# Windowed attention, mixture of experts and MLP: local values loaded once, with a product in two passes over alternating key halves

## Chip, cores and metric

One core of a Trainium2 chip. The metric is the device time of one execution in microseconds; of several runs the median is given.

## What is computed

Four batches of 576 positions, eight heads of 64. In heads 0 to 3 a query sees its own key and the 31 before it; in heads 4 to 7 every fourth position back, 32 of them (`rel` is query minus key position):

```
scores = scale * q @ k.T
mask   = (0 <= rel < 32)                  if h < H // 2
         (0 <= rel < 128, rel % 4 == 0)   otherwise
x      = softmax(where(mask, scores, -1e9)) @ v        # heads side by side: (B, S, 512)
```

Behind it come a causal attention of four experts, of which each token takes the two with the highest gate logits, and a layer norm with an MLP (512 to 2048 to 512, relu) and a residual sum:

```
for e in range(4): out += w_e * softmax(causal(scale * (x@wq[e]) @ (x@wk[e]).T)) @ (x@wv[e]) @ wo[e]
y = out + relu(norm(out) * g @ w_ch1) @ w_ch2
```

All data are float32.

## The kernel before

**Local attention** works by head pair (two heads, one in each half of the 128 partitions), 4 pairs for each of 4 batches, 16 in all. Pairs 0 and 1 are plain, pairs 2 and 3 dilated; a dilated head is split into its four classes of position modulo 4, each of 144 positions, which then look like the plain case.

For each pair `load_qk` (line 330) loads queries and keys into two tiles `nat`, `load_v` (line 354) the values into a tile `vt`, and `turned_qk` (line 432) turns queries and keys by matmuls with an identity (`ptr`, line 451) into `qT` and `kT`, with 32 zero columns ahead of the keys. Some of these tiles lie in `x2a`, the space that later holds the tokens.

Queries go in blocks of 32. A block sees 64 keys: its own 32 and the 32 before. `scores` (line 497) writes for each block a matmul with a mask (lines 513 to 518) and one of queries with those 64 keys (line 526), on eight tiles of 64 by 32 of TensorE's array at a time. `window` (line 532) takes maxima and exponentials, `local` (line 555) sums and normalises them on VectorE or GpSimd (line 578), turns them by matmuls (`ppt`, line 585) into `pT`, and multiplies them with the values (`po`, line 612) on four tiles of 64 by 64: one matmul for each block and head, with the 64 values that the block sees as weights and its 32 columns of `pT` streamed:

```
nc.tensor.matmul(pos[u][z, o:o + m], vv, pT[y, p0:p0 + m], start=True, stop=True)
```

For that, `vt` holds the values of every block with those of the block before it: each value is loaded twice. `u` is 0 or 1, for the first ten and the last eight or ten blocks. `rounded` (line 619) then splits the result into `xh` (ScalarE, line 633) and `xl` (VectorE, line 635).

**Behind it** `value_tile` multiplies with the experts' value weights (`pv`, line 659), `project` with query and key weights (`pp`, line 760), `attend` is the causal attention (`s` in lines 832 to 835, `ppt` in 908, `py` in 927 and 929), `out_proj` (`pwo`, line 985) gives the tokens. `attention_weights` (line 287) splits each weight that has landed into a rounded part (ScalarE, line 294) and a rest (GpSimd, line 296). The MLP (`phid`, line 1213, `pout`, line 1235) takes some 450 us at the end.

**The order** on every engine is set ahead of time by the kernel's own planner, `run_chains`: each piece of work is a chain that yields its operations with a supposed duration (`yield op("PE", 1050.0, ...)`), its need of a buffer (`acq`) or of an earlier result (`key`); what could start first by these suppositions is issued first, by rank where equal. SP issues all loads in the order of `all_loads` (line 411): after batch 0's queries, keys and values come the weights, then batch 1.

Of the kernel before, what the change touches and what calls it, by code (L numbers as in the profile page):

```python
# [23 lines left out]
def windowed_attention_moe_mlp(  # L24
# [37 lines left out]
    LEAN = 0.0  # L62

# [38 lines left out]
    HOME = list(range(8)) + [9, 10, 11, 12, 8, 13]  # L102
    LENT = 11
# [5 lines left out]
    def x2(ti):  # L109
        if ti < NTA:  # L110
            return x2a[:, HOME[ti]]
# [16 lines left out]

    mask = win.tile([P, NS, 2 * W], BF16, name="mask")
    nc.gpsimd.memset(mask[:, 1], 0.0)  # L130
    for x in range(4):
        m = mask[W * x:W * x + W, 1]
        nc.gpsimd.affine_select(out=m, in_=m, pattern=[[1, 2 * W]], compare_op=ALU.is_gt,
                                fill=NEG, base=0, channel_multiplier=-1)
        nc.gpsimd.affine_select(out=m, in_=m, pattern=[[-1, 2 * W]], compare_op=ALU.is_ge,
                                fill=NEG, base=W, channel_multiplier=1)
    for x in (0, 2, 3, 4):
        nc.vector.tensor_copy(mask[:, x], mask[:, 1])
    for x in range(4):
        nc.vector.memset(mask[W * x:W * x + W, x % 2 * 2, 0:W], NEG)  # L140
# [165 lines left out]
    places.update(nat=[0.0] * 2, vt=[(0.0, 8), (0.0, LENT), (0.0, 0), (0.0, 0)], qT=[0.0] * 2, xh=[0.0] * XB)  # L306
# [23 lines left out]
    def load_qk(b, hp, engines="SS"):  # L330
# [9 lines left out]
        for x, src in enumerate((q, k)):  # L340
            if lent:
                nat = x2a[:, 4 * hp - 4 + 2 * x:4 * hp - 2 + 2 * x].rearrange("p a n -> p (a n)")
            else:
                nat = win.tile([P, 2 * DM], F32, tag="nat", name="nat", bufs=2)
# [9 lines left out]
    def load_v(b, hp, engines=("SP",)):  # L354
# [3 lines left out]
        if home:  # L358
            vt = x2a[:, home:home + 3].rearrange("p a n -> p (a n)")[:, :4 * NS * D]
        else:  # L360
            vt = win.tile([P, 4 * NS * D], F32, tag="vt", name=f"vt{b}_{hp}", bufs=2)
        yield op("POOL", 1000.0 if dil else 250.0, [t])
        vs, jobs = v[b, h0], []
        if not dil:
            vt = vt.rearrange("p (i h d) -> p i h d", i=2 * NS, h=2)
            nc.gpsimd.memset(vt[0:W, 0], 0.0)
            jobs.append((16.0, vt[W:2 * W, 0], v[b, h0:h0 + 2, 0:W].rearrange("h p d -> p h d")))
            for u, i0, n in ((0, 1, 9), (1, 0, 8)):
                for h in range(2):
                    jobs.append((16.0 * n, vt[64 * u:64 * u + 64, i0:i0 + n, h],  # L370
                                 bass.AP(tensor=vs.tensor, offset=vs.offset + (h * S + (10 * u + i0 - 1) * W) * D,
                                         ap=[[D, 2 * W], [W * D, n], [1, D]])))
        else:
            vt = vt.rearrange("p (i h n) -> p i h n", i=NS, h=2)
            for u in range(NU):
                nc.gpsimd.memset(vt[64 * u:64 * u + W, 0], 0.0)
                nc.gpsimd.memset(vt[64 * u + W:64 * u + 2 * W, 4], 0.0)
            for u in range(NU):
                y, o = 64 * u, 2 * u * D
                for h in range(2):  # L380
                    jobs.append((70.0, vt[y:y + 2 * W, 1:4, h],
                                 bass.AP(tensor=vs.tensor, offset=vs.offset + h * S * D + o,
                                         ap=[[4 * D, 2 * W], [4 * W * D, 3], [1, 2 * D]])))
                for i, w0, w1 in ((0, W, 2 * W), (4, 0, CLS - 3 * W)):
                    jobs.append(((w1 - w0) * 0.7, vt[y + w0:y + w1, i],
                                 bass.AP(tensor=vs.tensor, offset=vs.offset + 4 * ((i - 1) * W + w0) * D + o,
                                         ap=[[4 * D, w1 - w0], [S * D, 2], [1, 2 * D]])))
        tv = 0.0
        for x, (kb, dst, src) in enumerate(jobs):
            ns = 470.0 if dil else 580.0  # L390
# [40 lines left out]

    def turned_qk(b, hp):
# [4 lines left out]
        qT = win.tile([P, S], F32, tag="qT", name=f"qT{b}_{hp}", bufs=2)  # L437
        kT = win.tile([P, W + S], F32, tag="kT", name=f"kT{b}_{hp}", bufs=2)
        yield op("POOL", 130.0, [tq])
        nc.gpsimd.memset(kT[:, 0:W], 0.0)  # L440
# [4 lines left out]
        for x in range(4):  # L445
# [11 lines left out]
            dst = kT[:, W:] if x > 1 else qT  # L457
# [30 lines left out]
    def piece(dil, u, s, c):  # L488

        i = 2 * NS * u + 2 * s + c  # L490
        if not dil:
            return W * i, W, 2 * W, 2 * W * s + W * c
        r, g = divmod(i, 5)
        m = min(W, CLS - W * g)
        return CLS * r + W * g, m, m + W, CLS * (r % 2) + W * g

    def scores(b, hp):
# [8 lines left out]
        t = yield op("PE", 1200.0, [tq, ta], "eighths")  # L506
# [13 lines left out]
        for s in range(NS):  # L520
            for u, z, c in tiles:
                n = parts(dil, u)
                if s < n:
                    q0, mq, mk, _ = piece(dil, u, s, c)
# [3 lines left out]
        give("qT", t)  # L528
        PSC[b, hp] = banks, psv
# [25 lines left out]
    def local(b, hp):  # L555
# [41 lines left out]
        t = yield op("PE", 1050.0, ends + [ta, tv], "quarters")  # L597
        for s in range(NS):
            for c in range(2):
                for u in range(NU):  # L600
                    if s >= parts(dil, u):
                        continue
                    _, m, _, o = piece(dil, u, s, c)
                    y = slice(64 * u, 64 * u + 64)
                    for h, z in enumerate(HALVES):
                        p0 = P * s + side(u, z).start + W * c
                        if dil:
                            r, g = divmod(2 * NS * u + 2 * s + c, 5)
# [717 lines left out]
```

## Time and profile before

| | |
|---|---|
| median of 3 runs | 730.36 us (729.48 to 731.95) |
| profiled execution | 730.35 us |
| its span | 728.6 us |
| TensorE busy | 702.5 us, 96% |
| VectorE, ScalarE, GpSimd busy | 506.0, 287.1, 156.6 us |
| moved by DMA | 45.49 MB |

The span goes from the first to the last instruction of that execution. Busy time of TensorE counts matmuls that overlap as one stretch. A float32 matmul leaves two records in the trace. The granted clock is 1.00 at 2.4 GHz and 0.50 at 1.2 GHz.

### The profile page before, as it was taken

Reading aid. Unit: us, or ns where it says so; the run is one execution under the profiler, and the core shown is the slowest. Engines: PE = TensorE matmul, PEld = TensorE weight load, DVE = VectorE, ACT = ScalarE, POOL = GpSimd, SP = SyncE. Lnnn points to the kernel's source line nnn. Section 1 sums busy time; section 2 is a strip of 40 time slices with the busy share of each in tenths; the row PEclk is TensorE's granted clock in tenths of the full one; section 3 lists DMA queues with packets and bytes.
Section 4 is the critical chain, followed back from the end, with each engine's and each line's share of the span. In section 5 each row is a group of like instructions: output and inputs, shape, how many; then the busy total and the mean of one; then the engine's idle time right before and its main releaser. Section 6 shows DMA issues by size and latency. Waiting matters only on the chain.

```text
span 728.6 us, 16135 instructions
## 1 busy us (share of the span) xinstructions
PE 702.5 (96%) x6483; PEld 592.5 (81%) x6483; DVE 506.0 (69%) x1206; ACT 287.1 (39%) x814; POOL 156.6 (21%) x209
## 2 busy tenths in 40 slices
PE   6977999999999899999999999999999999999997
PEld 4876998998898878778888888888888888888886
DVE  4526789976978889994958984684674864854343
ACT  3445567756766665962412231221221211311100
POOL 3352101010100204430404341240330420410000
PEclk9577799999999999999999999999999999999999
DMA  9699165125612111110101220020110110100123
GB/s 156 126 177 165 36 132 112 50 52 104 117 23 68 38 42 47 37 48 0 58 1 59 73 72 30 29 61 26 58 58 0 59 58 2 57 1 0 58 88 115
DMA packets 89275, 45.49 MB, mean 62 GB/s; under 512 B 65648, under 2 KB 84592, under 8 KB 89200
## 3 DMA queue, kind: packets, MB, share of 16 engines
q1 hardware_dynamic: 89200, 44.46, 26.4%
q8 instruction: 51, 0.84, 0.5%
q14 instruction: 24, 0.20, 0.1%
HBM read 37.37 MB, written 4.72 MB: 58 GB/s over the span
## 4 chain that ended last, share of the span: by engine, by line
PE 85%; DVE 9%; SPq 2%; ACT 2%; DMA 1%; issue 1%; POOL 0%; DVEq 0%; ACTq 0%; POOLq 0%
PE pout L1235 27%; PE phid L1213 27%; PE pp L760 6%; PE pv L659 4%; PE po L612 3%; PE pwo L985 3%; PE ptr L451 2%; PE ppt L908 2%; PE py L929 2%; SPq L322 2%; PE s L526 2%; PE py L927 1%; PE s L832 1%; PE s L833 1%; PE ppt L585 1%; DMA x2a<-in_k_dram 1%
## 5 line engine op out<-in xcount | busy, mean ns | idle before, releaser
L1213 PE MATMUL phid<-xn,wp 128*128 128x512 f32 (+1 forms) x960 | 219.9, 372 | 0.0
L1235 PE MATMUL pout<-wp,ht 128*128 128x512 f32 x864 | 217.9, 394 | 0.0
L1213 PEld LDWEIGHTS phid<-xn,wp 128*128 128x128 f32 x960 | 168.3, 188 | 34.1 <-issue 0.2
L1235 PEld LDWEIGHTS pout<-wp,ht 128*128 128x128 f32 x864 | 160.7, 188 | 36.2 <-issue 0.3
L1244 DVE SCALAR_TENSOR_TENSOR x2a<-pout,rstd,x2a 128x512 f32<-128x512 f32 x124 | 92.2, 748 | 55.8 <-PE pout L1235 54.9
L1218 ACT ACTIVATE ht<-phid 128x512 fp32r<-128x512 f32 (+1 forms) x80 | 44.5, 556 | 215.3 <-PE phid L1213 215.3
L1220 DVE SCALAR_TENSOR_TENSOR ht<-phid,ht 128x512 fp32r<-128x512 f32 (+1 forms) x80 | 50.7, 634 | 60.5 <-ACT ht L1218 60.1
L1087 POOL TENSOR_TENSOR d_pw<-d_pw,d_t 128x512 f32<-128x512 f32 x32 | 41.4, 1294 | 217.2 <-DVE d_pw L1084 185.7
L1099 POOL TENSOR_TENSOR wp<-d_pw,wp 128x512 fp32r<-128x512 f32 x32 | 42.6, 1330 | 40.7 <-ACT wp L1097 40.7
L1071 ACT ACTIVATE d_sq<-ws 128x512 f32<-128x512 f32 x32 | 21.6, 676 | 52.9 <-DVE d_pw L1090 29.2
L578 POOL TENSOR_TENSOR sc<-sc,rs 128x384 f32<-128x384 f32 (+2 forms) x20 | 14.6, 738 | 106.2 <-DVE rs L571 53.8
L1097 ACT CAST wp<-d_pw 128x512 fp32r<-128x512 f32 x32 | 20.0, 624 | 40.6 <-DVE d_pw L1090 33.1
L848 ACT ACTIVATE Pp<-s,nm 128x448 f32<-128x448 f32 (+3 forms) x64 | 30.6, 478 | 13.2 <-DVE nm L846 10.6
L245 ACT COPY pT<-ppt 128x256 f32<-128x256 f32 (+3 forms) x63 | 27.0, 434 | 17.3 <-PE ppt L908 9.2
L832 PE MATMUL s<-KH,SQ 128*128 128x288 f32 (+4 forms) x96 | 31.5, 333 | 0.3 <-ACT G L245 0.2
L1090 DVE SCALAR_TENSOR_TENSOR d_pw<-d_sq,d_pw 128x512 f32<-128x512 f32 x32 | 22.0, 688 | 13.9 <-POOL d_pw L1087 13.8
L846 DVE TENSOR_REDUCE nm<-s 128x1 f32<-128x448 f32 (+3 forms) x64 | 26.2, 416 | 6.3 <-PE s L835 5.9
L1244 DVE SCALAR_TENSOR_TENSOR x2b<-pout,rstd,x2b 128x512 f32<-128x512 f32 x32 | 24.0, 749 | 9.3 <-PE pout L1235 9.1
L908 PE MATMUL ppt<-ident,Pp 128*128 128x128 f32 x160 | 29.2, 285 | 1.1 <-DVE xn L1175 0.8
L833 PE MATMUL s<-klz,SQ 128*128 128x288 f32 (+4 forms) x96 | 28.7, 303 | 0.0
L1077 DVE SCALAR_TENSOR_TENSOR d_t<-ws,d_t 128x512 int32<-128x512 int32 x32 | 27.6, 861 | 0.5
L551 ACT ACTIVATE sc<-s,mx 128x64 f32<-128x64 f32 x97 | 21.7, 330 | 14.8 <-DVE mx L542 11.9
(171 smaller groups left out, 1284.4 us busy)
## 6 DMA issues: line engine op xcount, KB each, us to landing
ws<-in_moe_w_ch_dram SPq DMA_DIRECT2D x32, 512.0 KB, 3.6
nat<-in_q_dram SPq DMA_DIRECT2D x12, 288.0 KB, 3.8
nat<-in_k_dram SPq DMA_DIRECT2D x12, 288.0 KB, 4.3
out_dram<-x2a SPq DMA_DIRECT2D x12, 256.0 KB, 2.1
KH<-KH SPq DMA_DIRECT2D x32, 72.0 KB, 2.7
vt<-in_v_dram SPq DMA_DIRECT2D x12, 144.0 KB, 4.2
vt<-in_v_dram SPq DMA_DIRECT2D x12, 128.0 KB, 5.5
x2a<-in_v_dram SPq DMA_DIRECT2D x16, 96.0 KB, 4.2
```

What stands on the lines that cost most here:

```text
L760: nc.tensor.matmul(pp[:, :HS], ws[:, c, pr_ * P:(pr_ + 1) * P], xs[:, c, cs], start=n == 0, stop=n == 3 * KC - 1)
L832: nc.tensor.matmul(ps[:m, :z - a], SQ[ee][:, q0:q0 + m], KH[ee][:, a:z], start=True, stop=False)
L833: nc.tensor.matmul(ps[:m, :z - a], SQ[ee][:, q0:q0 + m], KL[ee][:, a:z], start=False, stop=not end)
L848: nc.scalar.activation(Pt[:m, :n], pss[0][:m, :n], AF.Exp, bias=nm[:m, ee:ee + 1], accum_out=sm[:m, ee:ee + 1])
L908: nc.tensor.transpose(pt[:, P * (j - 1):P * j], Ps[ee][:, k0:k0 + P], ident)
L1087: nc.gpsimd.tensor_tensor(pf, pf, t1.bitcast(F32), op=ALU.add)
L1099: nc.gpsimd.tensor_tensor(lo, pf, hi.bitcast(F32), op=ALU.subtract)
L1213: nc.tensor.matmul(ph[:, :n_tok], ws[:, c * P:(c + 1) * P], xs[c], start=n == 0, stop=n == 3 * KC - 1)
L1218: nc.scalar.activation(hh[:, :n_tok], ph[:, :n_tok], AF.Relu)
L1220: nc.vector.scalar_tensor_tensor(hl[:, :n_tok], ph[:, :n_tok], 0.0, hh[:, :n_tok].bitcast(F32), op0=ALU.max, op1=ALU.subtract)
L1235: nc.tensor.matmul(po, a_[:, sl], w_, start=n == 0, stop=n == 3 * len(fs) - 1)
L1244: nc.vector.scalar_tensor_tensor(x2(i), po, rstd[:, i:i + 1], x2(i), op0=ALU.mult, op1=ALU.add)
```

## The change

Values are loaded once: `vt` holds, for the plain pairs, slots of 64 positions (for `u` = 1 beginning two blocks early), and for the dilated ones three slots for each class. So a block of 32 keys lies in partitions 0 to 31 of a half if its number is even, in 32 to 63 if odd. The scores put the 64 keys of a block in the order that fits this: for even blocks the two groups of 32 are swapped by a reversed read of `kT`, and the masks are built to match. The product becomes two passes, one over even key blocks and one over odd, which add up in PSUM: each matmul has one block of 32 keys as its weights (both heads' 64 value columns, or in the odd pass pieces of 32) and streams the two query blocks that see it, 64 columns.

`qT` and `kT` become two lasting pairs with the zero columns written once; `nat` gets a third tile; `vt` is smaller, and two more of its places lie in `x2a`, which loses its permutation `HOME`. The planner's suppositions change with it: 900 for 1200 (scores), 850 for 1050 (product), and those of the issues.

```
+    VW = 6 * P
...
-    HOME = list(range(8)) + [9, 10, 11, 12, 8, 13]
-    LENT = 11
+    LENT = 12
...
-    places.update(nat=[0.0] * 2, vt=[(0.0, 8), (0.0, LENT), (0.0, 0), (0.0, 0)], qT=[0.0] * 2, xh=[0.0] * XB)
+    places.update(nat=[0.0] * 3, vt=[(0.0, 8), (0.0, 10), (0.0, LENT), (0.0, 0), (0.0, 0)], qT=[0.0] * 2, xh=[0.0] * XB)
...
-            vt = vt.rearrange("p (i h d) -> p i h d", i=2 * NS, h=2)
-            nc.gpsimd.memset(vt[0:W, 0], 0.0)
-            jobs.append((16.0, vt[W:2 * W, 0], v[b, h0:h0 + 2, 0:W].rearrange("h p d -> p h d")))
-            for u, i0, n in ((0, 1, 9), (1, 0, 8)):
+            vt = vt[:, :NS * 2 * D].rearrange("p (i h d) -> p i h d", i=NS, h=2)
+            for u in range(NU):
                 for h in range(2):
-                    jobs.append((16.0 * n, vt[64 * u:64 * u + 64, i0:i0 + n, h],
+                    jobs.append((80.0, vt[64 * u:64 * u + 64, :, h],
...
-            vt = vt.rearrange("p (i h n) -> p i h n", i=NS, h=2)
-            for u in range(NU):
-                nc.gpsimd.memset(vt[64 * u:64 * u + W, 0], 0.0)
-                nc.gpsimd.memset(vt[64 * u + W:64 * u + 2 * W, 4], 0.0)
+            vt = vt.rearrange("p (i h n) -> p i h n", i=3, h=2)
             for u in range(NU):
                 y, o = 64 * u, 2 * u * D
                 for h in range(2):
-                    jobs.append((70.0, vt[y:y + 2 * W, 1:4, h],
+                    jobs.append((45.0, vt[y:y + 2 * W, 0:2, h],
...
-                for i, w0, w1 in ((0, W, 2 * W), (4, 0, CLS - 3 * W)):
-                    jobs.append(((w1 - w0) * 0.7, vt[y + w0:y + w1, i],
+                jobs.append((11.0, vt[y:y + CLS - 4 * W, 2],
...
+    QKT = [(win.tile([P, S], F32, name=f"qT{x}"), win.tile([P, W + S + W // 2], F32, name=f"kT{x}")) for x in range(2)]
...
-                    nc.tensor.matmul(psv[u][k:k + mq, s, :mk], qT[z, q0:q0 + mq], kT[z, q0:q0 + mk],
+                    keys = kT[z, q0:q0 + 2 * W].rearrange("p (a w) -> p a w", a=2)
+                    nc.tensor.matmul(psv[u][k:k + mq, s], qT[z, q0:q0 + mq], keys[:, ::-1] if swap else keys,
                                      start=False, stop=s == n - 1)
...
-        t = yield op("PE", 1050.0, ends + [ta, tv], "quarters")
+        t = yield op("PE", 850.0, ends + [ta, tv], "halves")
+        for odd in range(2):
...
+                    for g in range(odd - 2 if odd and u and not dil else odd, n, 2):
+                        kk = min(W, CLS - W * g) if dil else W
+                        sl = g // 2 if dil else g // 2 + u
+                        jobs[u].append((sl, r, kk, OW * r + W * max(g, 0), at[max(g, 0):g + 2]))
+            for x in range(max(map(len, jobs))):
                 for u in range(NU):
...
+                    y0 = 64 * u + W * odd
+                    dw = W if odd else D
+                    for d0 in range(0, 2 * D, dw):
...
+                        nc.tensor.matmul(pos[u][d0:d0 + dw, o:o + W * len(at)], vv, pp, start=not odd and not x,
+                                         stop=bool(odd) and x == len(jobs[u]) - 1)
```

The planner orders much anew. Two places are shown.

ScalarE, batch 0, where the key weights are cast (`wkh`, then `wqh`), before:

```order
L245 COPY pT<-ppt 128x384 x2
L245 COPY pT<-ppt 128x256
L294 CAST wkh<-ws_att 128x256 x3
L633 CAST xh_138<-po 128x2x144 x2
L294 CAST wkh<-ws_att 128x256
L294 CAST wqh<-ws_att 128x256 x2
L633 CAST xh_138<-po 128x2x144 x2
L294 CAST wqh<-ws_att 128x256 x2
```

and now:

```order
L255 COPY pT<-ppt 128x384
L255 COPY pT<-ppt 128x256
L304 CAST wkh<-ws_att 128x256
L255 COPY pT<-ppt 128x384
L304 CAST wkh<-ws_att 128x256 x2
L255 COPY pT<-ppt 128x256
L304 CAST wkh<-ws_att 128x256
L304 CAST wqh<-ws_att 128x256
L655 CAST xh_160<-po 128x2x144 x2
L304 CAST wqh<-ws_att 128x256 x3
L655 CAST xh_160<-po 128x2x144 x2
```

The casts of the key weights stood ahead of the rounding (`xh`) of the third pair, with all copies of `pT` done; now they stand between the copies of `pT`, and the first query weight ahead of that rounding.

TensorE, batch 1. Before, from the end of the second pair's scores on:

```order
L526 MATMUL s_1101<-kT_1_947,qT_1_946 32x64 x4
L585 MATMUL ppt<-ident,sc_132 128x128 x5
L612 MATMUL po<-pT,vt_0_819 64x32 x36
L451 MATMUL ptr<-ident,x2a 128x72 x16
L585 MATMUL ppt<-ident,sc_133 128x128 x3
```

Now a group of `ptr` (sixteen, of the third pair) and that pair's scores follow the second pair's scores directly, and then come:

```order
L782 MATMUL pp<-xh_160,wqh 128x288
L782 MATMUL pp<-xl_161,wqh 128x288
L782 MATMUL pp<-xh_160,wql 128x288
L456 MATMUL ptr<-ident,nat 128x72 x4
L590 MATMUL ppt<-ident,sc_154 128x128 x3
L456 MATMUL ptr<-ident,nat 128x72 x4
L590 MATMUL ppt<-ident,sc_155 128x128 x3
L590 MATMUL ppt<-ident,sc_154 128x128 x2
L456 MATMUL ptr<-ident,nat 128x72 x4
L590 MATMUL ppt<-ident,sc_155 128x128 x2
```

The transposes of the exponentials (`ppt`) followed the scores at once, with the product behind them; now the third pair's transposes and scores and six projection matmuls (`pp`) stand between, and the fourth pair's `ptr` among the `ppt`.

## Rows read from the trace of the kernel before

**Rows 1.** Busy time by stage: window, length, busy (instructions), granted TensorE clock, DMA, GB/s

```profile
0.00:50.00 50.00, 38.03 (x784) 31.90 (x785) 20.56 (x54) 20.97 (x63) 20.18 (x60) 0.73 0.88 151
50.00:110.00 60.00, 55.55 (x976) 50.67 (x976) 42.78 (x137) 35.55 (x122) 12.67 (x30) 0.85 0.64 117
110.00:240.00 130.00, 128.89 (x2243) 114.16 (x2242) 110.50 (x374) 88.50 (x299) 13.47 (x33) 1.00 0.36 73
```

**Rows 2.** Waits of TensorE, 0 to 110 us: total, times, longest

```profile
PE po L612 <- DVE xl L635: 4.1, 1, 4.1
PE ppt L585 <- POOL sc L578: 2.5, 2, 2.2
PE ptr L451 <- DMA x2a<-in_q_dram: 2.3, 1, 2.3
```

**Rows 3.** All engines by time around 42 us: start, length, idle before, releaser

```profile
40.01 1.49 ACT L294 CAST wkh<-ws_att 128x256 fp32r<-128x256 f32 x3 [3.74 <-DMA ws_att<-in_moe_wk_dram]
...
41.41 1.19 ACT L633 CAST xh<-po 128x288 fp32r<-128x288 f32 x2
...
42.85 2.32 PE L612 MATMUL po<-pT,x2a 64*64 64x32 f32 x76 [4.15 <-DVE xl L635]
```

**Rows 4.** SP's DMA issues by time

```profile
5.33 4.03 SPq L322 DMA_DIRECT2D vt<-in_v_dram  x5
...
12.04 4.48 SPq L322 DMA_DIRECT2D vt<-in_v_dram  x5
...
24.74 11.56 SPq L322 DMA_DIRECT2D x2a<-in_v_dram  x16
36.34 2.95 SPq L282 DMA_DIRECT2D ws_att<-in_moe_wk_dram  x4
```

**Rows 5.** Busy time by five microseconds, columns as in rows 1

```profile
10.00:15.00 5.00, 2.09 (x91) 1.60 (x91) 3.63 (x10) 3.25 (x15) 1.36 (x3) 1.00 1.19 166
...
35.00:40.00 5.00, 3.70 (x104) 3.40 (x102) 0.72 (x2) 0.79 (x2) 0.00 (x0) 1.00 0.55 135
...
45.00:50.00 5.00, 5.00 (x27) 4.96 (x26) 1.33 (x2) 1.85 (x5) 3.25 (x8) 0.50 1.20 167
...
70.00:75.00 5.00, 5.00 (x168) 4.60 (x168) 2.92 (x6) 2.27 (x9) 0.00 (x0) 0.50 0.91 139
```

**Rows 6.** TensorE by time: passes of scores and product at half and full clock

```profile
24.28 2.35 PE L612 MATMUL po<-pT,vt 64*64 64x32 f32 x72
...
29.25 1.34 PE L526 MATMUL s<-kT,qT 64*32 64x64 f32 x80
...
83.60 1.36 PE L612 MATMUL po<-pT,x2a 64*64 64x32 f32 x80
...
185.86 0.96 PE L526 MATMUL s<-kT,qT 64*32 64x64 f32 x72
186.75 0.33 PE L891 MATMUL ph<-ident,Ph 128*128 128x128 f32 x1
187.01 1.35 PE L612 MATMUL po<-pT,x2a 64*64 64x32 f32 x72
```

**Rows 7.** DMA issues of local values: engine, count, KB each, us to landing

```profile
vt<-in_v_dram SPq DMA_DIRECT2D x12, 144.0 KB, 4.2
vt<-in_v_dram SPq DMA_DIRECT2D x12, 128.0 KB, 5.5
```

**Rows 8.** TensorE by time after the second scores of batch 1

```profile
63.03 0.91 PE L585 MATMUL ppt<-ident,sc 128*128 128x128 f32 x5 [2.17 <-POOL sc L578]
64.31 2.35 PE L612 MATMUL po<-pT,vt 64*64 64x32 f32 x72 [0.38 <-DVE pT L245]
66.59 2.18 PE L451 MATMUL ptr<-ident,x2a 72*128 72x72 f32 x16
```

**Rows 9.** Lines 612 and 526: duration of one record in ns, least, median, most

```profile
L612 PE MATMUL po<-pT,vt x752: 206/219/313, 17.9 to 222.5; 64*64 64x32 f32 x173, 64*64 64x16 f32 x15
...
L526 PE MATMUL s<-kT,qT x1216: 202/216/314, 8.1 to 223.6; 64*32 64x64 f32 x153, 64*16 64x48 f32 x21
```

More of the change, by code (lines that the diff above doesn't have):

```diff
@@ L127, in side, with band @@
         return HALVES[1 - HALVES.index(z)] if u else z
+    def band(m, swap):
+        own, prev = (m[:, :W], m[:, W:]) if swap else (m[:, W:], m[:, :W])
+        nc.gpsimd.affine_select(out=own, in_=own, pattern=[[-1, W]], compare_op=ALU.is_ge,
+                                fill=NEG, base=0, channel_multiplier=1)
+        nc.gpsimd.affine_select(out=prev, in_=prev, pattern=[[1, W]], compare_op=ALU.is_gt,
+                                fill=NEG, base=0, channel_multiplier=-1)
     mask = win.tile([P, NS, 2 * W], BF16, name="mask")
@@ L132, in windowed_attention_moe_mlp @@
         m = mask[W * x:W * x + W, 1]
[L133 to L136, printed above, removed]
+        band(m, x % 2 == 0)
     for x in (0, 2, 3, 4):
         nc.vector.tensor_copy(mask[:, x], mask[:, 1])
-    for x in range(4):
-        nc.vector.memset(mask[W * x:W * x + W, x % 2 * 2, 0:W], NEG)
+    for x in (0, 2):
+        for s in (0, 2):
+            nc.vector.memset(mask[W * x:W * x + W, s, W:], NEG)
+    for x in (1, 3):
+        m = mask[W * x:W * x + W, NS - 1]
+        nc.gpsimd.memset(m, 0.0)
+        band(m, True)
     tri = const.tile([P, E, E], F32, name="tri")
@@ L430, in all_loads @@
                     yield from load_weights(3)
+    QKT = [(win.tile([P, S], F32, name=f"qT{x}"), win.tile([P, W + S + W // 2], F32, name=f"kT{x}")) for x in range(2)]
+    for _, kT in QKT:
+        nc.gpsimd.memset(kT[:, :W], 0.0)
+        nc.gpsimd.memset(kT[:, W + S:], 0.0)
     def turned_qk(b, hp):
@@ L436, in turned_qk @@
         tq = yield acq("qT")
[L437 to L440, printed above, removed]
+        qT, kT = QKT.pop(0)
         dil = 2 * hp >= H // 2
@@ L596, in local @@
         pos = [bank("po") for _ in range(NU)]
-        t = yield op("PE", 1050.0, ends + [ta, tv], "quarters")
-        for s in range(NS):
-            for c in range(2):
+        t = yield op("PE", 850.0, ends + [ta, tv], "halves")
+        OW = 5 * W
+        for odd in range(2):
+            jobs = [[], []]
+            for u in range(NU):
+                n = 2 * parts(dil, u)
+                for r in range(2 if dil else 1):
+                    if dil:
+                        n, at = 5, [P * (2 * r + g // 2) + W * (g % 2) for g in range(4)] + [P * (NS - 1) + W * r]
+                    else:
+                        at = [P * (g // 2) + W * (g % 2) for g in range(n)]
+                    for g in range(odd - 2 if odd and u and not dil else odd, n, 2):
[3 more added lines that the diff above has]
+            for x in range(max(map(len, jobs))):
@@ L600, in local @@
                 for u in range(NU):
-                    if s >= parts(dil, u):
+                    if x >= len(jobs[u]):
                         continue
[L603 to L608, printed above, removed]
-                            vv = vt[y, g, h, D * (r % 2):D * (r % 2) + D]
-                        else:
-                            vv = vt[y, 2 * s + c, h]
-                        nc.tensor.matmul(pos[u][z, o:o + m], vv, pT[y, p0:p0 + m], start=True, stop=True)
+                    sl, r, kk, o, at = jobs[u][x]
```

49 lines of the change are left out of this document (27 added, 22 removed).

## Prediction

> **What bounds the kernel now.** The profiled execution took 730.35 us, 1.75 us more than its span of 728.6; the median of the three timed runs is 730.36, so its rows and the runs tell of the same time. I read the busy table by stage first. TensorE is busy for 128.9 of the 130 us from 110 to 240 us, at full clock, but for only 38.0 of the first 50 us at a mean clock of 0.73, and for 55.6 of the next 60 at 0.85 [rows 1]. So there are two kinds of stage. In the first 110 us some 16 us are idle and much of the rest runs at half clock: what comes earlier there is time won. From 110 us on TensorE is full, and a microsecond added to its work is a microsecond lost.
>
> Next the waits of TensorE in the first 110 us: the longest is 4.1 us of the product behind VectorE's rounding, then 2.5 us behind GpSimd's normalising and 2.3 us for queries from DMA [rows 2]. The list of all engines around the first shows what is behind it. ScalarE waits 3.74 us for the key weights to land and casts them until 41.5; only then comes the rounding of the third head pair (xh at 41.41), then VectorE's xl, and the product of the fourth pair, which needs those PSUM banks, starts at 42.85 after 4.15 us [rows 3]. The weights are late because of SP's queue: their four issues start at 36.34, behind sixteen issues of local values that take 11.56 us, and behind two earlier groups of five with 4.03 and 4.48 us [rows 4]. The stall also costs clock: it was 1.00 from 35 to 40 us, and 0.50 from 45 to 50, where TensorE was busy throughout [rows 5].
>
> **The change part by part: loads.** A head pair's values were five issues (plain) or eight (dilated), and are four or six. Ahead of the key weights stand two plain and two dilated pairs: 2 x 1 + 2 x 2 = 6 issues fewer. At the mean price of such an issue (4.03/5 = 0.81, 4.48/5 = 0.90, 11.56/16 = 0.72 [rows 4]) that is 0.81 + 0.90 + 4 x 0.72 = 4.6 us. If the price followed the bytes (560 to 320 KB per plain pair, 544 to 288 KB per dilated one) the 20.07 us of these groups would be 2.30 + 2.56 + 6.12 = 10.98, so 9.1 us less. I take 4.6, as the issues are there whatever their size, and keep both ends. With the weights 4.6 us earlier they land ahead of need, since ScalarE had waited 3.74 us. In the new order ScalarE casts the first key weights ahead of the last copies of pT, so a remaining delay would hit the product again; between, TensorE has 18 value matmuls as cover. I count the 4.1 us as gone. What is late next there is TensorE's own work.
>
> With the stall goes the half clock behind it: 5.0 us of dense work at 0.50 would be 2.5 us at full clock [rows 5], and the product pass of that place took 2.32 us where the same pass at full clock takes 1.36 [rows 3, 6], 0.96 more. Together 3.5 us; the other end is 0, if the clock falls for another reason.
>
> The third pair's queries: TensorE waits 2.3 us for them [rows 2], behind values of the first pair, which shrink by 2 x 144 + 2 x 128 + 16 - 320 = 240 KB [rows 7] (16 KB by the shape of the fifth). At 166 GB/s [rows 5] that is 1.4 us. I take that; by the issue alone it is 0.81.
>
> Batch 1: after its second scores TensorE waits 2.17 us for GpSimd's sc, and 0.38 us for pT [rows 8]. The new order puts sixteen transposes, the third pair's scores and six projection matmuls between; such transposes took 2.18 us there [rows 8], so with the rest I count 2.55 us as covered. The condition is that the third pair has landed: its loads stand behind 6 + 2 issues fewer. If the cover is not there, the 2.55 us come back.
>
> **The product.** A plain pair took 36 matmuls of 64 rows and 32 columns (72 records, as float32 makes two each), and takes 18 (even: 32 rows, weights 64 wide, 64 columns) and 40 (odd: weights 32 wide): 116 records. A dilated one goes from 80 to 24 + 32 matmuls, 112 records. No row shows the new shapes, so I price them by the nearest. At full clock a pass of 72 took 1.35 us; less the 0.21 us of one matmul [rows 9] that is 15.8 ns per record, and 14.4 for the dilated one (1.36 us, 80) [rows 6]. The scores have weights 32 wide and 64 columns on eight tiles, like the odd pass: (0.96 - 0.20)/72 = 10.5 ns. Even records have the width of weights of the old product, so I give them its price. Plain: 36 x 15.8 + 80 x 10.5 ns = 1.41 us against 1.14, so +0.27. Dilated: 48 x 14.4 + 64 x 10.5 = 1.36 against 1.15, so +0.21. Mean +0.24. A second form of tile inside the pass adds one more change of form: between the transpose at 186.75 and the product at 187.01 lie 0.26 us [rows 6], of which some 0.11 is the transpose's own, so 0.15. Sum +0.39 us per pass; ten of the sixteen passes (one for each batch and head pair) start from 83.6 us on, where TensorE is full: +3.9. At half clock the old pass has (2.35 - 0.21)/72 = 29.7 ns and the scores (1.34 - 0.20)/80 = 14.3 [rows 6]: 36 x 29.7 + 80 x 14.3 = 2.21 against 2.14, with the change of form +0.2 to +0.25; six early passes, most at half clock, give +1.4. **Product: +5.3 us.** Ends: all new records at 10.5 ns and no price for the change of form, 1.22 and 1.18 us against 1.14 and 1.15, so +0.05 a pass and +0.9 in all; or even records at twice the price for twice the columns (below).
>
> The page "TensorEngine Tiling (Array Packing)" of the Trainium skill, under Key Properties, says that a change of tiling mode drains the engine; the 0.15 us above is what a row shows of it here.
>
> **Edits at nothing.** The scores keep their count; keys are read as two blocks, in half of them backwards. The trace has no such read; were it as dear as the product's record, 76 x 5.3 ns would be 0.4 us a pass, 6.4 in all, but the columns and tiles are the same, so I take 0 and keep this end. GpSimd loses its memsets of vt and kT and gets a few masks ahead of the first dilated scores; it is not waited for there. The third tile of queries and keys lets SP issue earlier; from 110 us on TensorE does not wait for loads, so 0.
>
> **Sum.** -4.1 - 3.5 - 1.4 - 2.55 + 5.3 = -6.3 us: 730.35 - 6.3 = **724.0 us**. This case's own range is 718 to 728.
>
> **Rivals.** *Larger gain.* From 65 to 83 us TensorE is dense again but at half clock (0.50 at 70 to 75 [rows 5]), after the stalls around 60. If the denser order holds the clock, half of 18 us is won as well: 724 - 9 = 715. For it: the fall follows those stalls. Against it: work as dense as that did not bring the clock back for 18 us. Chance 0.18.
>
> *The lead is given back.* The new order wants the second and third pair of batch 1 sooner; DMA is busy for 0.91 from 70 to 75 us even now [rows 5]. If transposes wait 2 to 3 us for each and the clock falls again, 2 x 3 us bring it to 730. VectorE at 110.5 of 130 us [rows 1] could hold the lead back too. Chance 0.16.
>
> *Slower: streamed columns set the product's price.* If the 15.8 ns are the 32 columns on four tiles, an even record with 64 costs 31.6: plain 36 x 31.6 + 80 x 10.5 = 1.98 us, dilated 32 x 28.8 + 16 x 14.4 + 64 x 10.5 = 1.82, with the change of form +0.99 and +0.82 a pass, 14.5 us in all, against 11.6 won: 733; with part of the lead lost, 736. It decides from 11.6/16 = 0.73 us a pass. Against it: the scores stream 64 columns on twice the tiles in less than 15.8 ns. A price per record that the width doesn't lower goes the same way: 116 x 15.8 and 112 x 14.4 ns give +0.73 with the change of form, 11.7 in all, and eat the whole gain. Chance 0.22.
>
> The page "TensorE: Matmul & The Clock Gate", in the section "Wait — 56ns, not 53.3ns?", has a floor of about 25 ns from one matmul's start to the next, however small. By it 44 and 32 more records would add some 0.95 us a pass and the time would be 736, as an estimate. The trace disagrees: records follow each other here in 10.5 to 15.8 ns, so it adds nothing to that chance.
>
> **How the numbers follow.** Forecast 0.44, larger gain 0.18, given back 0.16, slower 0.22. About 0.3% (2.2 us) is what a measurement of this kernel can tell from no change. Faster is the first two, 0.62; same 0.16; slower 0.22. The range leaves out the best part of the larger gain and the worst of the product's price, 0.2 together: 713 to 736.
>
> **What would show it.** Right: the key weights' issues start 4 to 9 us earlier; no wait of the product behind xl; clock above 0.5 between 42 and 50 us; one pass at full clock at 1.6 to 1.8 us where it was 1.35; the idle time of TensorE before 110 us near 10 us. Wrong: passes of 2 us or more, DMA as releaser of the transposes of batch 1, or a new wait of ScalarE behind the weights' casts.

## The result, and the profile after

The changed kernel takes 733.88 us (median of 20 runs, 728.22 to 738.48), the kernel before 729.81 us (20 runs, 726.24 to 731.95): the ratio is 1.0054, with a 95% interval of 1.003 to 1.0078. It is slower by half a per cent where 6.3 us of gain were forecast. The profiled execution took 735.07 us, its span is 733.3.

The page of the profile, busy time and instructions of each engine, and the queue that brings instructions (packets, MB, share):

```profile
PE 707.0 (96%) x7091; PEld 595.6 (81%) x7091; DVE 502.8 (69%) x1200; ACT 288.5 (39%) x800; POOL 153.8 (21%) x171
...
q8 instruction: 56, 0.92, 0.5%
```

TensorE is busy 4.5 us longer (702.5 before), and idle for 26.3 us where it was idle for 26.1. So nothing was won in idle time, and what the product costs stands uncovered. Busy time by stage, columns as in [rows 1]:

```profile
0.00:50.00 50.00, 42.99 (x945) 35.78 (x946) 20.99 (x55) 22.61 (x67) 18.25 (x53) 0.93 0.83 146
50.00:110.00 60.00, 54.60 (x1206) 49.66 (x1206) 42.65 (x139) 36.01 (x121) 9.00 (x12) 0.89 0.48 96
110.00:240.00 130.00, 123.51 (x2392) 109.98 (x2391) 99.89 (x335) 81.45 (x266) 12.63 (x18) 0.99 0.25 54
```

Before 110 us the idle time fell from 16.4 to 12.4 us, but 2.9 us of that are no gain. The clock's record in this trace begins at 34.7 us; ahead of it the view puts 1.00, so the 0.93 of the first row is no reading. The lengths of the matmul records tell more. Scores up to 16 us, before, after, and in e9 (below), whose code is that of the kernel before up to 517 us (least, median and longest ns):

```profile
L526 PE MATMUL s<-kT,qT x144: 212/216/241, 8.1 to 12.5; 64*32 64x64 f32 x144
L530 PE MATMUL s<-kT,qT x144: 281/311/313, 8.3 to 13.4; 64*32 64x64 f32 x144
L526 PE MATMUL s<-kT,qT x144: 280/311/313, 8.3 to 13.3; 64*32 64x64 f32 x144
```

311 ns is what these records take in the kernel before between 22 and 31 us, at a granted clock of 0.50; before, this stretch ran at 1.00. From 6 to 16 us TensorE is busy 5.91 us before, 8.77 after and 8.38 in e9, for 200, 199 and 194 records. So an execution can begin at half clock without any change of the code: it fills idle time with longer records, and costs little (the 500th record starts at 29.5 us before and at 29.7 in e9).

From 110 to 240 us, where TensorE had been full [rows 1], it is now idle for 6.5 us, 5.4 more than before. The waits of TensorE over the whole span say for what:

```profile
PE s L530 <- issue: 6.9, 4, 2.3
...
PE po L633 <- DVE xl L657: 1.6, 2, 1.4
...
PE po L633 <- issue: 1.2, 1, 1.2
...
PE pwo L1007 <- issue: 0.4, 1, 0.4
```

Of the waits that the forecast wanted gone, the 4.1 us behind xl are 1.6, the 2.5 behind GpSimd's sc [rows 2] are 0.6, and the 2.3 for queries are no longer there. This last is not shown to be won by the change: in e9 they are 0.7. All waits with a releaser add up to 13.5 us (20.2 before, 16.7 in e9). In their place stands "issue", idle time for which the profile shows no releaser: 8.5 us, against 1.2 before (two waits of the scores). So: +4.5 busy, +7.3 issue, -6.7 other waits, and -0.4 that the view doesn't list, make the 4.7 us of the span. Against e9 less its added row, which begins at half clock too, the first three are +3.6, +6.4 and -3.2.

SP's issues, answering to [rows 4]: the key weights' start 5.9 us earlier, at 30.47.

```profile
4.86 3.44 SPq L332 DMA_DIRECT2D vt<-in_v_dram  x4
...
10.17 3.98 SPq L332 DMA_DIRECT2D vt<-in_v_dram  x4
...
21.59 8.84 SPq L332 DMA_DIRECT2D x2a<-in_v_dram  x12
30.47 3.10 SPq L292 DMA_DIRECT2D ws_att<-in_moe_wk_dram  x4
```

Of the 5.9 us the values' own issues make 3.8 (20.07 became 16.26); the other 2.1 come from other issues that got shorter, most of them of queries and keys.

TensorE by time (start, length, tile and shape, count, idle before). The product of one pair is followed at once by the scores of another, and inside these lies the new wait:

```profile
120.13 1.71 PE L633 MATMUL po<-pT,vt 32*64 32x64 f32 x116
...
122.62 0.91 PE L530 MATMUL s<-kT,qT 64*32 64x64 f32 x70 [0.52 <-issue]
...
123.47 0.72 PE L530 MATMUL s<-kT,qT 64*32 64x64 f32 x48
126.35 0.46 PE L530 MATMUL s<-kT,qT 64*32 64x64 f32 x32 [2.16 <-issue]
126.74 0.43 PE L913 MATMUL ph<-ident,Ph 128*128 128x128 f32 x1
```

A pass of the product takes 1.71 us at full clock, where it took 1.35 [rows 6]: that price was forecast. The scores behind it wait for no data, buffer or engine that the view shows, and stop twice in the middle. In windows of a quarter of a microsecond the queue of instructions shows one packet of 16 KB at 120.0, one at 123.5 and one at 127.25 us. Its packets follow the count of TensorE's instructions (matmuls and weight loads): 51 packets for 2 x 6483 before, 56 for 2 x 7091 now, some 254 each. In none of the eighteen traces are two packets nearer than 3.25 us, and where many short records stand together they come every 3.3 to 4 us. A packet is worth 127 matmul records with their weight loads; at the 10 to 15 ns of a record here it is used up in 1.3 to 1.9 us.

Where the stops lie says the same. Each row goes from 0 to the end of one of the six (length, TensorE's busy time and its records so far, clock, DMA share, GB/s; the clock with the gap told above):

```profile
0.00:22.64 22.64, 17.71 (x346) 1.00 0.98 155
0.00:75.71 75.71, 64.63 (x1484) 0.91 0.70 128
0.00:122.61 122.61, 109.70 (x2369) 0.92 0.60 112
0.00:126.34 126.34, 111.27 (x2497) 0.92 0.59 110
0.00:185.63 185.63, 168.25 (x3507) 0.94 0.50 93
0.00:210.87 210.87, 192.82 (x4141) 0.94 0.46 88
```

From stop to stop there are 1138, 885, 128, 1010 and 634 records: 9, 7, 1, 8 and 5 times 126 to 128, one packet's worth. The two stops of the kernel before come after 347 and 978 records, five packets apart. So where TensorE stops without a releaser, it is at the border between two packets, whatever matmul stands there; it goes on 2.1 to 3.1 us after a packet's start.

### The profile page after: what moved, and what is told of

It reads as the page before. It is cut to its first block, busy times and chain, and to the rows that moved or that the text cites. A ratio compares the mean times of both kernels' runs of the same rounds, so it can differ in the third digit from the quotient of the medians.

```text
span 733.3 us, 17227 instructions
## 1 busy us (share of the span) xinstructions
PE 707.0 (96%) x7091; PEld 595.6 (81%) x7091; DVE 502.8 (69%) x1200; ACT 288.5 (39%) x800; POOL 153.8 (21%) x171
## 4 chain that ended last, share of the span: by engine, by line
PE 83%; DVE 11%; ACT 3%; issue 2%; DMA 1%; POOL 0%; SPq 0%; POOLq 0%; DVEq 0%; ACTq 0%
PE pout L1257 27%; PE phid L1235 27%; PE pp L782 5%; PE po L633 4%; PE pv L681 4%; PE pwo L1007 2%; PE ppt L930 2%; PE ptr L456 2%; PE s L530 2%; PE ppt L590 2%; PE py L951 2%; PE s L854 1%; PE py L949 1%; PE s L855 1%; DVE Pp L905 1%
## 5 line engine op out<-in xcount | busy, mean ns | idle before, releaser
L1257 PE MATMUL pout<-wp,ht 128*128 128x512 f32 x864 | 220.4, 395 | 0.0
L255 ACT COPY pT<-ppt 128x384 f32<-128x384 f32 (+3 forms) x59 | 25.5, 440 | 20.0 <-PE ppt L590 10.1
L657 DVE TENSOR_TENSOR xl<-po,xh 128x288 fp32r<-128x288 f32 (+2 forms) x32 | 16.9, 565 | 18.2 <-ACT xh L655 18.1
L530 PE MATMUL s<-kT,qT 64*32 64x64 f32 (+1 forms) x1216 | 18.1, 250 | 9.0 <-issue 6.9
```

The costliest lines, as they stand in the source:

```text
L530: nc.tensor.matmul(psv[u][k:k + mq, s], qT[z, q0:q0 + mq], keys[:, ::-1] if swap else keys, start=False, stop=s == n - 1)
L1257: nc.tensor.matmul(po, a_[:, sl], w_, start=n == 0, stop=n == 3 * len(fs) - 1)
```

## Experiments

**Theory A**: TensorE runs out of instructions where hundreds of short records follow each other. **Theory B**: the product and the new order as such are too dear. **Theory C**, from the second group on: the planner's new suppositions are at fault. Each kernel is compared with runs of the kernel before on the same chip; the numbers follow the order in which they ran. Waits are those of the execution profiled.

**e3: without the odd pass.** The loop `for odd in range(2)` runs once; the odd key blocks are missing from the output.

> The changed kernel without the odd pass of the product (the odd key blocks are left out of the sum); order and loads unchanged, 36 or 48 records a pass in place of 116 or 112. Theory A: the passes get 0.8 to 1.0 us shorter at full clock (10 of 16), about 1.3 at half, and the idle time by 'issue' falls from 8.5 to under 3 us: 712 to 718 us. Theory B: the passes' own time alone, 9 us and some of the early 6: 719 to 725 us.

716.89 us, ratio 0.9808 (0.9778 to 0.9839): the time is where A put it, the issue waits, 3.9 us in all, are above its 3. Product of both kernels and waits of this one (columns of the first row: window, length, busy of TensorE with count, weight loads, VectorE, ScalarE, clock, DMA share, GB/s; the tile po alone):

```profile
0.00:330.00 330.00, 15.27 (x672) 13.25 (x672) 16.86 (x32) 15.33 (x32) 0.95 0.34 72
...
PE s L530 <- issue: 3.1, 2, 1.9
PE ptr L456 <- DMA x2a<-in_q_dram: 2.7, 1, 2.7
```

The same row reads 30.65 for the changed kernel and 26.62 before. Two things follow. The odd pass costs 15.4 us of records and 4.6 us of issue waits (all of them are 3.9 us here). And this kernel, whose product is 11.4 us shorter than before, is only 13.7 us faster than before: all other edits together bring some 2 us here, 2.7 us of issue waits more than before among them. This execution began at full clock (the first scores take 216 ns), and waits for the third pair's queries at 14.8 us as the kernel before does at 15.0: with the loads of the change this wait is no shorter.

**e2: more records in the kernel before.** 20 (plain) or 16 (dilated) of the product's matmuls in each pass are followed by one of 2 columns with the same operands.

```
+                        for _ in range(1 if s < (3 if not dil else 2) and not (s == 2 and c) else 0):
+                            nc.tensor.matmul(pos[u][z, o:o + 2], vv, pT[y, p0:p0 + 2], start=True, stop=True)
```

> The kernel before, with 20 (plain) or 16 (dilated) of the product's matmuls in each pass issued a second time for two columns: 40 or 32 records more a pass, about as many as the change adds (44 or 32), with hardly any columns, and the same results. Loads, values and suppositions are those of before. Theory A: the time rises by 16 passes x 0.4 to 0.6 us of records and by 2 to 6 us of idle time by 'issue': 738 to 744 us. Theory B: records alone, at most 16 x 0.5 us where TensorE is full: 733 to 738, idle time by 'issue' still 1 to 2 us.

743.16 us, ratio 1.0182 (1.0137 to 1.0226). The old order and the old product get the new waits as soon as there are as many records, 9.7 us in all where A expected 3 to 7, the most of it in the product (the execution profiled, at 750.85 us, is the longest of the six):

```profile
PE po L612 <- issue: 8.6, 5, 3.2
```

It answers the rival on streamed columns too. A pass of 112 records takes 1.88 us at full clock (87.80 to 89.68) where 80 took 1.36 [rows 6]: 16 ns for each added record of 2 columns, as much as the 14.4 to 15.8 of those with 32.

**e9 and e10: the supply by itself.** The kernel before, with 640 records that depend on nothing, in one row or in eight, ahead of groups of the MLP. The edit of e9 (in e10 the condition is `BN[0] % 10 == 0`, and 40 stands for 320):

```
+            if BN[0] == 40:
+                for j in range(320):
+                    z, u, c = 64 * (j % 2), j // 2 % 2, 32 * (j // 4 % 2)
+                    k = (64 - z if u else z) + c
+                    nc.tensor.matmul((bx if u else ph)[k:k + 32, :64], w1h[z:z + 64, c:c + 32].bitcast(F32),
+                                     xnh[0][z:z + 64, :64].bitcast(F32), start=True, stop=True)
```

> The kernel before with 320 small float32 matmuls (weights 64 by 32, 64 columns, on eight tiles as in the scores; 640 records, 1280 instructions with their weight loads) put in one row ahead of one group of the MLP's first layer, where TensorE is full and no DMA, buffer or other engine is waited for; their results are overwritten. At the 10.5 ns that a record of the scores takes they are worth 6.7 us. Theory A: five blocks of 256 instructions can't come nearer than some 3.5 us each, so the row takes 15 to 19 us, 8 to 12 of it idle with no releaser, and the time is 743 to 750 us. Theory B (no limit of that kind; the idle times of the changed kernel come from somewhere else): the row takes 6.5 to 9 us and the time is 735 to 739 us.

> The same 320 matmuls as eight rows of 40 (80 records each, as a pass of scores), one ahead of every tenth group of the MLP's first layer, some 50 us apart. Theory A: each row finds its instructions fetched, so hardly any idle time with no releaser is added; 6.7 us of records and 8 x 0.3 us for two changes of form each give 736 to 741 us, at least 5 us less than the one long row. Theory B: the same as the one long row or some 2 us more.

One row: 744.7 us, ratio 1.0212 (1.0164 to 1.026). Eight rows: 738.63, ratio 1.0136 (1.0087 to 1.0184). Both are where A put them, and the same work differs by 6.1 us. The tile `extra` (half of the added matmuls) in e9, its waits, and stretches of 2 us around it (TensorE's busy time and count, clock, DMA share, GB/s):

```profile
L1217 PE MATMUL extra<-xn,wp x320: 212/307/313, 517.2 to 533.2; 64*32 64x64 f32 x160
...
PE extra L1217 <- issue: 7.4, 4, 2.2
...
518.00:520.00 2.00, 1.59 (x163) 1.00 0.04 8
520.00:522.00 2.00, 0.34 (x36) 1.00 0.00 0
522.00:524.00 2.00, 1.45 (x113) 0.60 0.63 133
524.00:526.00 2.00, 0.34 (x28) 0.50 0.35 137
526.00:528.00 2.00, 1.70 (x123) 0.50 0.04 8
```

and in e10, where no wait stands ahead of it:

```profile
L1217 PE MATMUL extra<-xn,wp x320: 216/216/240, 369.2 to 728.6; 64*32 64x64 f32 x160
```

In one row the 640 records run for 16.3 us (517.14 to 533.44), in spurts of 128 that begin 2.3 to 2.9 us after the packets of instructions at 519.0, 522.75, 526.75 and 530.5 us, and the clock falls to 0.50 on the way. The next packet starts 1.1 to 1.7 us after the records go on. The two add up to the 3.5 to 4 us from packet to packet, in which 128 records are worked off that need 1.3 us at 10.5 ns each: with its price, a limit of one packet in some 3.75 us is shown. The idle time, 7.4 us, is somewhat less than the 8 to 12 expected. The Trainium skill, "Runtime: NRT & Kernel Launch", in the section "Instruction fetch mechanics", says that instructions are refilled in blocks of 256, the next one fetched while the current one runs, and that this is mostly hidden. The size agrees with the 254 per packet here; "hidden" doesn't hold for rows of short matmuls, as 7.4 us here and 8.1 us in the changed kernel's scores and products show.

**e1, e5, e6: other work between the passes.** The planner gets a token `code` that a pass of scores or product takes and gives back some time after its end: 2 us in e1; 2.5 us in e6, with truer durations; in e5 the even and the odd pass are two pieces, with 1.5 us behind each and 2.5 us behind the scores.

```
+        tc = yield acq("code")
-        t = yield op("PE", 900.0, [tq, ta], "eighths")
+        t = yield op("PE", 900.0, [tq, ta, tc], "eighths")
+        give("code", t + 2000.0)
```

> The changed kernel, with one edit in the planner: a pass of scores or of the product may be planned only 2 us (supposed) after the last one, so that other work comes between. Instructions, data and prices are the same. Theory A (instruction supply: TensorE runs out of instructions when passes of hundreds of short records follow each other; 8.5 us idle by 'issue' in the changed kernel, 1.2 before): the idle time by 'issue' falls below 3 us, and the time from about 734 to 724 to 729 us. Theory B (the price of the two passes and an order in which VectorE and ScalarE come late cost the time, and the idle 'issue' is incidental): 731 to 737 us, as the passes cost the same.

> The changed kernel with the even and the odd pass of each product planned as two pieces of work and 1.5 to 2.5 us of other work wanted between any two of even pass, odd pass and scores. Theory A (TensorE's instructions arrive in blocks of 256, no two of them closer than some 3.5 us, so that scores and products that stand together run out of them): idle time of TensorE with nothing that the profile shows as releaser falls from 8.5 to under 4 us, no two blocks of the instruction queue nearer than 3.25 us, and the time is 725 to 731 us, some 2 us dearer than without the stalls because the form of tile changes more often. Theory B (the product's records and the new order as such are too dear): the idle time falls but the time stays at 733 us or above.

> The changed kernel with 1000 and 1700 ns supposed for scores and product (about what they take at full clock) and 2.5 us of other work wanted between any two of these passes. Theory A: idle time of issue under 4 us, time 724 to 731 us. Theory B: 733 us or above. The wider spacing of 2 us tried before (on suppositions that were too short, so that the passes began some 2.9 us apart by plan) brought no gain; if this one doesn't either, spacing whole passes costs more elsewhere than the supply.

A's times were missed by all three: 743.45 us, ratio 1.016 (1.0122 to 1.0197), above both theories; 759.7, 1.0418 (1.0388 to 1.0447), and 743.05, 1.0199 (1.0171 to 1.0227), both where B put them. In e1 the waits, 7.9 us in all, mostly moved into the product:

```profile
PE po L637 <- issue: 4.7, 5, 1.6
```

In e5 and e6 they fell, from 8.5 to 4.5 and 3.0 us, and others came, 32.0 and 24.5 us in all where the changed kernel has 13.5. The longest of e5, then of e6:

```profile
PE ptr L456 <- DMA nat<-in_q_dram: 5.3, 2, 4.6
```

```profile
PE ppt L592 <- DVE sc L585: 6.1, 2, 4.6
```

Holding a pass back delays what stands behind it; and the granted clock is 0.51 from 245 to 266 us in e5 and 0.50 from 232 to 248 in e6, where the changed kernel has 1.00. So these runs don't show what the time would be without the waits alone, and their times don't decide for B.

**e4: the same spacing in the kernel before**, 1.5 us.

> The kernel before, with the same edit of the planner (1.5 us, the longest at which this kernel's chains get along like in the first). Theory A: there is little idle time by 'issue' to win (1.2 us): 727 to 731 us. Theory B says the same; if it gains over 4 us, spacing helps by another way than the supply of instructions, and run e1 does not speak for A.

726.69 us, ratio 0.995 (0.9922 to 0.9979), just below what was expected. It is the one kernel of the study with a whole product whose interval lies below both, by little: the order alone moves the old kernel by half a per cent. Its issue waits are 1.3 us where before had 1.2, so supply is not why.

**e7, e8, e14, e15: the planner's suppositions.** Only the two durations that the planner supposes are changed.

```
-        t = yield op("PE", 900.0, [tq, ta], "eighths")
+        t = yield op("PE", 1200.0, [tq, ta], "eighths")
...
-        t = yield op("PE", 850.0, ends + [ta, tv], "halves")
+        t = yield op("PE", 1050.0, ends + [ta, tv], "quarters")
```

> The changed kernel with the planner's suppositions of before (1200 and 1050 ns for scores and product). Theory A: the order still puts 98, 98, 112 and 116 matmuls of scores and product together, so 4 to 8 us of issue idle stay and the time is 729 to 737 us. Theory C (the new suppositions and the order they make are at fault): 729 us or less, with the idle time of issue as in the changed kernel.

> The kernel before with the suppositions of the change (900 and 850 ns for scores and product), nothing else. Theory A: at most 76 matmuls stand together, issue idle under 3 us, time 726 to 732 us. Theory C: 733 us or above.

> The changed kernel with 1000 and 1700 ns supposed for scores and product, about what they take at full clock, and no spacing. Theory C (the suppositions are at fault): 730 us or less. Theory A: passes of 98, 116, 96 and 92 matmuls still stand together, the idle time with no releaser stays at 5 to 9 us, and the time is 731 to 737 us.

> The changed kernel with 1200 ns supposed for the scores as before, and 1700 for the product. If what the run with the suppositions of before won came from supposing the passes longer, this one is at 727 to 731 us too; if it came by the chance of one order, it is at 732 us or above. Theory A alone: at 116 and 116 matmuls in a row 5 to 9 us of idle time with no releaser stay.

| scores, product (ns) | kernel | us | ratio to before (95%) | issue waits, other waits (us) |
|---|---|---|---|---|
| 1200, 1050 | before | 729.81 | | 1.2, 20.2 |
| 900, 850 | changed | 733.88 | 1.0054 (1.003 to 1.0078) | 8.5, 13.5 |
| 1200, 1050 | changed (e7) | 729.97 | 1.0006 (0.9984 to 1.0028) | 9.0, 9.5 |
| 1200, 1700 | changed (e15) | 729.77 | 1.001 (0.9976 to 1.0044) | 4.7, 14.7 |
| 1000, 1700 | changed (e14) | 745.25 | 1.0232 (1.0174 to 1.029) | 6.3, 23.7 |
| 900, 850 | before (e8) | 731.34 | 1.0032 (1.0004 to 1.0061) | 3.6, 16.9 |

The same computation lies between 730 and 745 us by two numbers that only set the order. With the suppositions of before the change is no slower than before. By the ranges set down C has none of these: e7 (729.97, C had 729 or less) and e8 lie where A put the times, with more issue waits than A named; e14 is above both; e15 is within the 727 to 731 us of "longer passes", which e14, with the same 1700, contradicts. So the new suppositions decide whether the change is slower, but there is no rule in it: the truest durations gave the slowest order. The issue waits don't follow: e7 wins 3.9 us and still has

```profile
PE s L530 <- issue: 5.1, 5, 1.6
PE s L516 <- issue: 2.8, 1, 2.8
...
PE po L633 <- issue: 1.1, 1, 1.1
```

9.0 us of them in all, where e14 has 6.3 and takes 15.3 us longer. In e14 the head of the list is GpSimd's normalising again:

```profile
PE ppt L590 <- POOL sc L583: 6.0, 3, 3.0
PE po L633 <- issue: 5.1, 4, 1.5
PE pwo L1007 <- ACT sc L553: 2.1, 1, 2.1
```

**e16: suppositions of before, and 0.5 us between passes.**

> The changed kernel with the suppositions of before and 0.5 us of other work wanted between any two passes; no more than 98 matmuls stand together but in one place with 112. If order and supply add up: idle time with no releaser under 5 us and 724 to 728 us, faster than the kernel before. If spacing costs elsewhere what it saves, as it did with 2 us and more: 730 to 740 us.

728.63 us, ratio 1.001 (0.9974 to 1.0047), on runs of before that scattered from 722.85 to 733.33. The issue waits are 5.3 us, 3.7 less than in e7; the time is 1.3 us less, within the measurement, and both the 724 to 728 us and the 5 us of waits were missed by little.

**e11: two tiles for queries and keys**, `bufs=3` and its places back to 2.

> The changed kernel with two tiles for queries and keys in place of three. As the prediction costed the third tile at nothing, it expects 732 to 736 us, the changed kernel's own time. If the third tile is what lets passes of scores run together (theory A's cause of the waits for instructions), the idle time with no releaser falls from 8.5 to under 5 us and the time to 727 to 731 us; if it is what brings the loads early, the time rises to 737 or more.

742.56 us, ratio 1.0171 (1.0131 to 1.0211): 8.7 us above the changed kernel, with 9.2 us of issue waits for 8.5. The range stood for loads that come late, but no wait for DMA is longer than 0.3 us and no new wait stands out; TensorE is busy 4.6 us longer (711.6), and at a lower clock where the changed kernel has 1.00:

```profile
180.00:240.00 60.00, 57.05 (x1062) 49.77 (x1068) 44.09 (x151) 39.13 (x130) 8.04 (x12) 0.94 0.26 59
240.00:300.00 60.00, 59.36 (x517) 51.66 (x501) 51.75 (x172) 38.84 (x117) 15.09 (x12) 0.95 0.14 39
```

Some or all of it may again be the order, which the planner makes anew; the run can't part the two. A third tile in the kernel before wasn't tried.

**e12: most issues of values given twice.**

```
             issue(e, dst, src)
+            if kb > 20.0 and (dil or x):
+                issue(e, dst, src)
```

> The changed kernel, its order kept, with three of the four issues of a plain pair's values and four of the six of a dilated pair's given twice in a row, so that it moves as many bytes of values as the kernel before. Two plain and two dilated pairs stand ahead of the key weights, 14 issues more at 0.75 to 0.95 us. The prediction's theory of the gain (fewer issues and bytes bring the weights early): they come 8 to 13 us later than in the changed kernel, the product waits 4 us or more behind the rounding again, and the time is 738 to 748 us. Rival: the loads were not what the early stage waits for, and the time stays within 731 to 737 us.

831.97 us, ratio 1.1408 (1.1357 to 1.1459), and no answer to the question: the second issue writes where the first does, and waits until it has landed. Seven issues of a plain pair take 12.11 us, 1.73 each in place of 0.86. The issues, and what SP waited for:

```profile
4.97 12.11 SPq L332 DMA_DIRECT2D vt<-in_v_dram  x7
...
67.47 2.07 SPq L292 DMA_DIRECT2D ws_att<-in_moe_wk_dram  x4
...
SPq L332 <- DMA vt<-in_v_dram: 71.8, 34, 3.7
```

**e13: more issues that wait for nothing**, into a tile `dump` with four places in turn.

```
+            if x < (2 if dil else 1):
...
+                issue(e, rows.rearrange("p (a n) -> p a n", a=1 if dil else 2), few)
```

> The changed kernel, its order kept, with one more issue of values for each plain pair and two for each dilated pair, 32 KB each, into a tile that nobody reads, so that they wait for nothing. Six of them stand ahead of the key weights, as many as the change took away. The prediction's step (0.72 to 0.90 us an issue on SP's queue, 4.6 us in all, and a stall of the product of up to 4.1 us with half clock behind it): the key weights' issues start 4 to 5.5 us later than in the changed kernel, at 35 to 36 us, the product waits 3 us or more behind the rounding, and the time is 736 to 742 us. Rival: TensorE has work enough there in the new order, and the time stays at 731 to 735 us.

736.12 us, ratio 1.0114 (1.0059 to 1.0168). The key weights start at 34.50, 4.0 us later and just short of the 35 to 36 expected, 0.67 us for each of the six issues. The time is 2.2 us above the changed kernel, at the low end of what was expected, and the two intervals overlap. The wait behind the rounding did not come back; there are waits for queries and keys (execution profiled: 740.12 us, the longest of the six):

```profile
34.50 2.08 SPq L292 DMA_DIRECT2D ws_att<-in_moe_wk_dram  x4
...
PE ptr L465 <- DMA x2a<-in_q_dram: 2.5, 2, 2.2
PE ptr L465 <- DMA nat<-in_q_dram: 2.5, 1, 2.5
...
PE po L642 <- DVE xl L666: 1.4, 1, 1.4
```

The 2.2 us stand at 14.3 us, where every execution that began at full clock has 1.5 us or more for these queries; only the 2.5 at 68.9 us, in batch 1, are new. So this run doesn't bear out the step from later weights to the stall.

## Why the prediction was wrong

**Loads, right in their time, not shown in their effect.** 4.6 us earlier was taken (4.6 to 9.1), 5.9 was measured, 3.8 of it by the values' own issues; one of these costs 0.86 to 1.00 us (3.44/4, 3.98/4) and 0.74 (8.84/12), and fewer bytes didn't make it cheaper. The waits that were to go made 8.05 us (4.1, 1.4, 2.55); the waits with a releaser fell by 6.7, but only by 3.2 against e9, which began at half clock as the changed kernel did. The 1.4 us for the third pair's queries were not won: e3, with the same loads and a start at full clock, waits 2.7 us for them where before waits 2.3. And that the earlier weights ended the stall behind xl is not shown: in e13 they come 4.0 us later again, and the wait stays at 1.4 us; the new order may have ended it.

**The half clock behind the stall, not found.** 3.5 us were taken, with 0 as the other end. From 40 to 50 us the granted clock is 0.66 where it was 0.51; but it is 0.66 in e9 too, where the stall stands as before, with 4.2 us. So the clock there need not hang on the stall, and the zero end is the one that the runs bear out. The busy time outside the product is 676.4 us where it was 675.9, with 2.9 us more of it in the slower start.

**The product, right.** 5.3 us were taken; the tile po is busy 4.0 us longer (30.65 against 26.62 us), and a plain pass takes 1.71 to 1.78 us at full clock where 1.35 + 0.27 + 0.15 = 1.77 was worked out. The rival on the price of streamed columns gave a time near the measured one, 733, by a mechanism that isn't there: no pass took 2 us or more at full clock, and in e2 records of 2 columns cost as much as those of 32.

**The step that failed** is the sum's pricing of 608 more records by their durations alone, under "The product". Its term for a full TensorE was only busy time; that the instructions themselves, twice 608 more of them, have to arrive stood nowhere. Before had a sign of it, 1.2 us of issue waits in two stops of the scores, and it wasn't read. The new waits are 7.3 us (6.4 against e9), and 7.8 in e7's order. With this term and 0 for the clock, the forecast's own numbers give -8.05 + 5.3 + 7.3 = +4.6; the spans differ by 4.7. That this comes so near is luck: waits and product came out smaller than taken (6.7 and 4.0), the two executions began at different clocks, and the order moves as much.

**The edits at nothing** were the other failure. Without the third tile, and in the order that goes with it, the time is 8.7 us longer (e11); and the suppositions, which the sum didn't price at all, decide whether the change is slower: -3.9 us with the old ones (e7). The rival "the lead is given back" put the time at 730 us, nearer than the forecast, but named DMA, which no long wait of the changed kernel shows.

**What stays open** is how much of the 4 us the waits for instructions cost and how much the order. The first are shown in place and size, by their distance in records, and by e9 against e10 as a mechanism; but every run that took them away changed the order too, e7 won 3.9 us without taking any away, and e15, with half of them gone, takes as long as e7.

## What to carry to other kernels

Count the instructions that a change adds and where they stand together, not only how long each takes: a pass split into more and smaller matmuls can be cheap by its records and still stop the engine, and idle time with no releaser, however short, is where to look for it before. Where a planner sets the order, its supposed durations are part of the change: run the new code with the old ones before judging either. And before two executions' first stretches are compared, look at how long the same records take in each: one may have begun at half clock.

## Not expected of the hardware

One packet of 16 KB of instructions, 254 of TensorE's, came no sooner than 3.25 us after the one before in any trace, and TensorE's stops lie a whole number of packets apart; 640 short records in one row cost 14.9 us (744.7 - 729.77) where the same in rows of 80 cost 8.9 with the changes of form (738.63 - 729.77). Behind the first stop of that row the clock fell from 1.00 to 0.50, between 522 and 524 us. And an execution can run from 6 to 16 us at half clock or at full clock with the same code (scores of 311 ns in e9, of 216 before).
